# Instruction order and PSUM banks of a fused attention and gated-MLP kernel: a stored table in place of a list scheduler

## Chip, cores and metric

The kernel runs on one NeuronCore of one Trainium2 chip. The metric is the device time of one execution in microseconds. An execution is a little longer than the span of its profile, which runs from the first to the last recorded instruction.

## The reference

```python
# q, k, v: batch 4, heads 8, sequence 1152, head size 64 (fp32)
q_pool = q.reshape(B, H, S // 2, 2, D).mean(axis=3)          # 576 pooled queries
scores = (1 / sqrt(D)) * q_pool @ k^T
attn = softmax(scores)
x = (attn @ v), heads side by side                           # 2304 tokens x 512
gate = sigmoid(x @ w_gate); val = x @ w_val                  # 512 -> 1536
out = (gate * val) @ w_out                                   # 1536 -> 512
```

## The kernel before

**Tiling.** 32 heads are worked in 16 pairs, and four pairs make a batch. The 576 pooled queries of a head fall into two halves of 288, and its 1152 keys into nine chunks of 128. For fp32 accuracy, operands are split into a high and a low fp32r part. A chunk of scores is two matmuls (L610) into one PSUM bank; the first works on `QA`, `KA`, the second on `QB`, `KB`, whose rows also subtract the row maximum. Row maxima come from separate products of 384 columns (L504; L412 for the first head; L504 on `KP`, `QP` for the last 64 queries of a pair), each reduced by VectorE (L510, L417), and are put into `QB` as a diagonal (L335).

**Attention.** In the first batch (heads 0 to 7) ScalarE makes one exponential per chunk (L614, tile `e`), and three chunks at a time are multiplied with `ve` in plain fp32 (L628). In the later batches it makes two, a rounded one into `eh` (L614) and an exact one in place in the bank (L643); VectorE forms the difference `el` (L646). `eh` and `el` are multiplied with `vt` in products of their own (L653, L657), accumulating in two banks. The sums of the exponentials are added up on GpSimd (L675 to L685) and brought in by the two matmuls of L730 on `dh`.

**Gated MLP.** `gated` works on one batch at a time: products of twelve matmuls of 288 columns (L846, in four operations of three each) with the weights `wg`, then with `wo`. ScalarE (tanh, L889), VectorE (L895, L931) and GpSimd (L903) finish them. The MLP of one batch runs beside the attention of the next; behind the last batch only MLP is left. Weights are converted once (`convert`), stored to HBM and loaded again each time by SyncE. Eighteen filler operations (`busy`, L949; four matmuls of 192 columns each, L951) depend on nothing but one memset.

**What sets the order.** Every piece of work is handed to a planner, `pl.op(engine, duration, function, priority, after, uses, take)`, and every buffer is a `Hold` of a tag with so many slots. `Plan.run` (L92) is a list scheduler: it starts the ready operation of the lowest priority number on each engine that is free, by hand-written durations, and gives a buffer the slot that is free the longest. `Plan.search` (L66, called at L1000) repeats this 30 times with shifted priorities. An operation counts as ready when all of `after` and the first user of each of its buffers are done; a buffer counts as free when all its users are done. The operations are then issued in the order found (L1001), under `manual_schedule`. The waits between engines are put in afterwards, from what each instruction reads and writes. TensorE, ScalarE, VectorE, GpSimd and SyncE (which issues nearly all DMAs) each run their own instructions in that order. The eight PSUM banks are the tag `b`; every other tag takes its slots in turn.

Of the kernel before, what the change touches and what calls it, by code (L numbers as in the profile page):

```python
# [22 lines left out]

class Op:
    def __init__(self, eng, dur, fn, prio, after=(), take=None, late=0.0, keep=0.0, behind=None):
        self.eng, self.dur, self.fn, self.prio = eng, dur, fn, prio
        self.after = [a for a in after if a is not None]
        self.take, self.late, self.keep = take, late, keep
        self.users, self.start, self.end, self.behind, self.next = [], None, None, behind, []


class Hold:


    def __init__(self, tag, first=None):
        self.tag, self.slot, self.ops = tag, None, []


class Plan:


    WAIT = 0.4
    LAT = {"PE": 0.2, "ACT": 0.16, "DVE": 0.14, "POOL": 0.1, "SP": 0.0}

    def __init__(self, slots, free_order=()):
        self.free_order = free_order
        self.ops = []
        self.slots = slots
        self.holds = {t: [] for t in slots}
# [6 lines left out]
    def op(self, eng, dur, fn, prio, after=(), uses=(), take=(), late=0.0, keep=0.0, behind=None):  # L56
        o = Op(eng, dur, fn, prio, after, list(take), late, keep, behind)
        for h in uses:
            if behind is None:
                o.after.append(h.ops[0])  # L60
        for h in list(take) + list(uses):
            h.ops.append(o)
        self.ops.append(o)
        return o

    def search(self, rounds, width, shift):  # L66
        dice = random.Random(1)
        best = self.run()
        end = max(o.end for o in best)
        made = [(o, o.start, o.end) for o in best]  # L70
        slots = [(h, h.slot) for hs in self.holds.values() for h in hs]
        for _ in range(rounds):
            at = dice.uniform(-width, end)
            near = [(o, o.prio) for o, s, _ in made if at <= s <= at + width and o.eng != "SP"]
            for o, p in near:
                o.prio = p + dice.uniform(-shift, shift)
            order = self.run()
            new = max(o.end for o in order)
            if new <= end:
                best, end = order, new  # L80
                made = [(o, o.start, o.end) for o in best]
                slots = [(h, h.slot) for hs in self.holds.values() for h in hs]
            else:
                for o, p in near:
                    o.prio = p
        for o, a, b in made:
            o.start, o.end = a, b
        for h, s in slots:
            h.slot = s
        return best  # L90

    def run(self):  # L92
        n_dep = {}
        ready = {e: [] for e in self.LAT}
        for o in self.ops:
            o.users, o.next = [], []
        for k, o in enumerate(self.ops):
            o.key = (o.prio, k)
            o.at = 0.0
            n_dep[o] = len(o.after)  # L100
            for a in o.after:
                a.users.append(o)
            if o.behind:
                n_dep[o] += 1
                o.behind.next.append(o)
        free = {t: [(0.0, s) for s in range(n)] for t, n in self.slots.items()}
        nxt = {t: 0 for t in self.slots}
        left, of = {}, {}
        for t, hs in self.holds.items():
            for k, h in enumerate(hs):  # L110
                h.k, h.end = k, 0.0
                left[h] = len(h.ops)
                for o in h.ops:
                    of.setdefault(o, []).append(h)
        for o in self.ops:
            if n_dep[o] == 0:
                heapq.heappush(ready[o.eng], (o.key, o))
        busy = {e: 0.0 for e in self.LAT}
        done, order, t = 0, [], 0.0
        times = [0.0]  # L120
        heapq.heapify(times)
        seen = set()

        def can(o, t):
            for h in o.take:
                n = sum(g.tag == h.tag for g in o.take) if h.tag in self.free_order else 1
                if (h.tag not in self.free_order and nxt[h.tag] != h.k) or sum(f <= t + 1e-9 for f, _ in free[h.tag]) < n:
                    return False
            return True

        while done < len(self.ops):
            if not times:
                left = sorted((o.key[0], o.eng) for e in ready for _, o in ready[e])
                raise RuntimeError(f"planner stuck at {t}: {left[:10]} {nxt}")
            t = heapq.heappop(times)
            while times and times[0] <= t + 1e-9:
                heapq.heappop(times)
            again = True
            while again:
                again = False  # L140
                for e in self.LAT:
# [896 lines left out]
```

## Time and profile before

| | |
|---|---|
| median of 3 runs | 920.66 us (920.31 to 920.88) |
| span of the profiled execution | 919.1 us |
| TensorE matmuls | 910.0 us busy, 99% of the span, 6371 instructions |
| TensorE weight loads | 882.8 us, 96% |
| VectorE / ScalarE / GpSimd | 71% / 72% / 73% |

The page lists no other time for the profiled execution than its span, so the difference between the median and the span, 1.6 us, is taken as what lies around the span. A matmul's recorded duration (about 295 ns for 288 columns) is longer than the distance from one start to the next (about 133 ns), because matmuls are pipelined. So the cadence, instructions per time, says more than the busy share.

### The profile page before, as it was taken

How to read it: one execution, taken by the hardware profiler on the slowest of the kernel's cores; microseconds unless marked ns; L12 is line 12 of the kernel's file. 1: busy time of each engine (PE TensorE's matmuls, PEld its weight loads, DVE VectorE, ACT ScalarE, POOL GpSimd, SP SyncE). 2: the span in 40 equal slices, each digit the busy share in tenths (PEclk: the TensorE clock that was granted, in tenths of full speed). 3: DMA queues.
4: the chain of work that ended last, by engine and by line, in shares of the span. 5: the costliest groups of instructions: out<-in, count | busy, mean ns of one | idle time of the engine just before them, and what ended most of it. 6: DMA issues, size and time to landing. Idle time of an engine off the chain costs nothing.

```text
span 919.1 us, 18605 instructions
## 1 busy us (share of the span) xinstructions
PE 910.0 (99%) x6371; PEld 882.8 (96%) x6371; DVE 649.5 (71%) x1427; ACT 657.5 (72%) x1703; POOL 671.1 (73%) x669
## 2 busy tenths in 40 slices
PE   8999999999999999999999999999999999999998
PEld 8888888999999999999999999999999999999998
DVE  6677779888898987878787878877777874510112
ACT  4798899989998886777887677677877767422111
POOL 6765366889888989889899888888889877521211
PEclk9999999999999999999999999999999999999999
DMA  6899888788868666555644455554545423435432
GB/s 140 212 289 247 275 254 261 239 266 273 262 210 275 206 202 192 161 157 149 166 136 142 131 157 157 160 148 132 166 123 158 142 93 115 166 139 183 162 115 75
DMA packets 57616, 166.27 MB, mean 181 GB/s; under 512 B 17393, under 2 KB 21745, under 8 KB 51377
## 3 DMA queue, kind: packets, MB, share of 16 engines
q1 hardware_dynamic: 57360, 164.78, 59.3%
q8 instruction: 50, 0.82, 0.4%
q10 hardware_dynamic: 160, 0.30, 0.1%
q14 instruction: 46, 0.37, 0.1%
HBM read 132.12 MB, written 23.59 MB: 169 GB/s over the span
## 4 chain that ended last, share of the span: by engine, by line
PE 91%; ACT 4%; DVE 3%; POOL 1%; DMA 1%; issue 1%; POOLq 0%; ACTq 0%; DVEq 0%
PE bank L846 47%; PE bank L610 15%; PE bank L504 7%; PE bank L628 7%; PE bank L657 6%; PE bank L653 6%; PE bank L730 1%; DVE pm L417 1%; PE bank L951 1%; DMA wg<-wg_d 1%; ACT eh L614 1%; ACT bank L643 0%; ACT KA L475 0%; DMA wo<-wo_d 0%; DVE el L646 0%
## 5 line engine op out<-in xcount | busy, mean ns | idle before, releaser
L846 PE MATMUL bank<-x,wg 128*128 128x288 f32 x2304 | 353.8, 295 | 0.0
L846 PEld LDWEIGHTS bank<-x,wg 128*128 128x128 f32 x2304 | 325.6, 188 | 1.1 <-ACT sg L889 0.4
L646 DVE TENSOR_TENSOR el<-bank,eh 128x288 fp32r<-128x288 f32 x432 | 192.9, 452 | 70.7 <-ACT bank L643 65.9
L510 DVE TENSOR_REDUCE pm<-bank 128x1 f32<-128x384 f32 (+1 forms) x375 | 199.7, 550 | 49.6 <-PE bank L504 45.0
L614 ACT ACTIVATE eh<-bank 128x288 fp32r<-128x288 f32 x432 | 176.4, 409 | 73.1 <-PE bank L610 65.9
L643 ACT ACTIVATE bank<-bank 128x288 f32<-128x288 f32 x432 | 176.9, 410 | 0.2
L610 PE MATMUL bank<-QA,KA 128*128 128x288 f32 x576 | 175.1, 308 | 1.5 <-DVE pm L510 0.9
L610 PE MATMUL bank<-QB,KB 128*128 128x288 f32 x576 | 167.4, 295 | 0.0
L903 POOL TENSOR_TENSOR g<-sg,g 128x288 fp32r<-128x288 f32 x96 | 79.9, 833 | 105.2 <-ACT g L899 102.7
L675 POOL TENSOR_TENSOR acc<-acc,eh 128x576 f32<-128x576 f32 x92 | 132.5, 1440 | 16.7 <-ACT eh L614 14.6
L846 PE MATMUL bank<-g,wo 128*128 128x288 f32 x864 | 139.2, 295 | 0.2
L657 PE MATMUL bank<-el,vt 128*128 128x288 f32 x432 | 127.2, 296 | 0.5 <-DVE el L646 0.5
L653 PE MATMUL bank<-eh,vt 128*128 128x288 f32 x432 | 127.3, 296 | 0.0
L846 PEld LDWEIGHTS bank<-g,wo 128*128 128x128 f32 x864 | 125.0, 188 | 1.2 <-DMA wo<-wo_d 0.3
L504 PE MATMUL bank<-KA,QA 128*128 128x384 f32 (+1 forms) x375 | 125.7, 350 | 0.2
L610 PEld LDWEIGHTS bank<-QA,KA 128*128 128x128 f32 x576 | 108.2, 188 | 5.9 <-DVE pm L510 1.3
L610 PEld LDWEIGHTS bank<-QB,KB 128*128 128x128 f32 x576 | 108.3, 188 | 1.3
L895 DVE SCALAR_TENSOR_TENSOR sg<-sg,bank 128x288 f32<-128x288 f32 x96 | 43.3, 451 | 81.2 <-PE bank L846 79.2
L657 PEld LDWEIGHTS bank<-el,vt 128*128 128x128 f32 x432 | 81.1, 188 | 1.5 <-DVE el L646 1.2
L653 PEld LDWEIGHTS bank<-eh,vt 128*128 128x128 f32 x432 | 81.1, 188 | 0.7 <-ACT eh L614 0.3
L675 POOL TENSOR_TENSOR acc<-eh,eh 128x576 f32<-128x576 f32 x48 | 68.7, 1431 | 15.6 <-ACT eh L614 10.9
L628 PE MATMUL bank<-e,ve 128*128 128x288 f32 x288 | 76.6, 407 | 0.0
(86 smaller groups left out, 1359.6 us busy)
## 6 DMA issues: line engine op xcount, KB each, us to landing
wg<-wg_d SPq DMA_DIRECT2D x48, 1024.0 KB, 5.2
wo<-wo_d SPq DMA_DIRECT2D x36, 512.0 KB, 3.9
kr<-in_kT_dram SPq DMA_DIRECT2D x62, 288.0 KB, 5.0
wg_d<-cs SPq DMA_DIRECT2D x24, 512.0 KB, 5.0
qr<-in_qT_dram SPq DMA_DIRECT2D x31, 288.0 KB, 4.1
KP<-KA SPq DMA_DIRECT2D x30, 288.0 KB, 4.4
vr<-in_v_dram SPq DMA_DIRECT2D x24, 288.0 KB, 3.1
cr<-in_wg_dram SPq DMA_DIRECT2D x12, 512.0 KB, 5.3
```

The lines of the kernel that those rows point to most:

```text
L504: nc.tensor.matmul(out=tl(m)[LO if t == 4 else ALL, 0:384], lhsT=lhs(t), rhs=rhs()[:, j * 384:(j + 1) * 384], start=True, stop=True)
L510: nc.vector.tensor_reduce(out=o, in_=tl(m)[p, 0:384], axis=AXX, op=ALU.max)
L610: nc.tensor.matmul(out=tl(m)[:, 0:GN], lhsT=tl(hd["k"])[k][:, ks], rhs=tl(hd["q"])[k][:, a:b], start=(k == 0), stop=(k == 1))
L614: nc.scalar.activation(out=ev(), in_=tl(m)[:, 0:GN], func=ACTF.Exp, scale=1.0 / 16.0)
L628: nc.tensor.matmul(out=tl(av[0])[:, 0:GN], lhsT=pair(c, 0), rhs=tl(h), start=(c == 0), stop=(c == NC - 1))
L643: nc.scalar.activation(out=p, in_=p, func=ACTF.Exp, scale=1.0 / 16.0)
L646: nc.vector.tensor_tensor(out=tl(el), in0=tl(m)[:, 0:GN], in1=ev().bitcast(F32), op=ALU.subtract)
L653: nc.tensor.matmul(out=tl(av[0])[:, 0:GN], lhsT=pair(c, w), rhs=ev(), start=(c == 0), stop=(c == NC - 1))
L657: nc.tensor.matmul(out=tl(av[1])[:, 0:GN], lhsT=pair(c, 1 - w), rhs=tl(el), start=(c == 0), stop=(c == NC - 1 and not mine_c))
L675: nc.gpsimd.tensor_tensor(out=tl(acc), in0=tl(old).bitcast(F32), in1=tl(eh).bitcast(F32), op=ALU.add)
L846: nc.tensor.matmul(out=ps[:, 0:GN], lhsT=l, rhs=r, start=(n == 0 and j == 0), stop=(n == 3 and j == 2))
L903: nc.gpsimd.tensor_tensor(out=g[:, 1, a:b], in0=tl(sg), in1=g[:, 0, a:b].bitcast(F32), op=ALU.subtract)
```

## The change

The scheduler is removed, and two constants take its place. Unpacked, `ORDER` holds 7153 numbers, a permutation of all operations as the code creates them; `PLACES` holds 3069 slots, one for each buffer hold. Operations, their instructions and their operands stay as they are, and so does the issue under `manual_schedule`, with waits derived from reads and writes.

Set against the order before, engine by engine: of TensorE's 3141 operations 3015 stand at another place, by 9 places on average and at most 62. Of ScalarE's 1703, 1486 are moved (4 places on average), of VectorE's 1348, 1185 (3), of GpSimd's 624, 544 (4), of SyncE's 337, 265 (2, at most 13). 1266 of 1448 PSUM holds sit in another bank; no slot of another tag differs. The order keeps to the true reads and writes and no longer to every `after` and buffer rule of the code. For instance, an `el` product may stand before the `eh` product of the same chunk, and a bank is taken by its first real writer.

```diff
-import heapq
-import random
+import base64
+import zlib
...
+ORDER = (
...
+)
+PLACES = (
...
+)
 class Op:
-    def __init__(self, eng, dur, fn, prio, after=(), take=None, late=0.0, keep=0.0, behind=None):
...
+    def __init__(self, eng, fn, after=()):
+        self.eng, self.fn, self.after = eng, fn, [a for a in after if a is not None]
...
     def op(self, eng, dur, fn, prio, after=(), uses=(), take=(), late=0.0, keep=0.0, behind=None):
-        o = Op(eng, dur, fn, prio, after, list(take), late, keep, behind)
-        for h in uses:
-            if behind is None:
-                o.after.append(h.ops[0])
+        o = Op(eng, fn, list(after) + [behind])
...
-    def search(self, rounds, width, shift):
...
-    def run(self):
...
+    def placed(self):
+
+        order = [self.ops[k] for k in unpack(ORDER, "H")]
+        holds = [h for t in self.slots for h in self.holds[t]]
+        for h, s in zip(holds, unpack(PLACES, "B"), strict=True):
             h.slot = s
+        assert len(set(order)) == len(self.ops) == len(order)
+        assert all(h.slot < self.slots[h.tag] for h in holds)
         return order
+
+
+def unpack(text, kind):
+    return list(memoryview(zlib.decompress(base64.b85decode(text))).cast(kind))
...
-    order = pl.search(30, 30.0, 1.0)
+    order = pl.placed()
     with tc.manual_schedule():
```

What the unpacked table says at the places of which the prediction speaks:

| | before | table |
|---|---|---|
| filler operations on TensorE ahead of the first maximum product (L412) | 8 | 15 |
| filler operations between the last L412 and the first score product | 4 | 0 |
| first-head reductions (L417) ahead of the first diagonal | 9 | 10 |
| `el` products with under 2.5 us of TensorE work between them and their scores, of 432 | 34 | 2 |
| the same distance for `el` / `eh` products, median | 3.0 / 2.7 us | 6.4 / 8.7 us |
| the same for L730 behind what its sums were made from, median | 6.2 us | 8.5 us |
| banks of a maximum product taken again within 1.25 us of TensorE work, of some 400 | 23 | 71 |
| smallest TensorE work between the last use of a `wg` buffer and its next use | 12.1 us | 6.8 us |
| the same for the last batch's `wo` tiles, which lie in `KA` | 5.2 us | 4.4 us |

"TensorE work" is counted along TensorE's order with the cadences of the trace (133 ns for 288 columns, 175 ns for 384, 242 ns for a plain fp32 matmul).

## Rows read from the trace of the kernel before

**Rows 1.** Page, its head and part 1: busy time, share of the span, instructions.
```profile
span 919.1 us, 18605 instructions
PE 910.0 (99%) x6371; PEld 882.8 (96%) x6371; DVE 649.5 (71%) x1427; ACT 657.5 (72%) x1703; POOL 671.1 (73%) x669
```
**Rows 2.** Page, part 4: the chain that ended last, by engine.
```profile
PE 91%; ACT 4%; DVE 3%; POOL 1%; DMA 1%; issue 1%; POOLq 0%; ACTq 0%; DVEq 0%
```
**Rows 3.** The same chain in order of time: start, length, what, count.
```profile
23.68 1.21 PE bank L504 x7
28.65 2.91 PE bank L628 x12
798.75 117.15 PE bank L846 x882
```
**Rows 4.** Groups by line: busy us, mean ns, idle before; for the counts.
```profile
L628 PE MATMUL bank<-e,ve 128*128 128x288 f32 x288 | 76.6, 407 | 0.0
L504 PE MATMUL bank<-KA,QA 128*128 128x384 f32 (+1 forms) x375 | 125.7, 350 | 0.2
L504 PE MATMUL bank<-KP,QP 128*128 128x384 f32 x45 | 15.6, 356 | 0.0
L412 PE MATMUL bank<-KA,QA 128*128 128x384 f32 (+1 forms) x15 | 3.9, 346 | 0.0
L951 PE MATMUL bank<-sel 128*128 128x192 f32 x72 | 12.5, 334 | 2.7 <-DVE sel L991 2.7
```
**Rows 5.** Busy time of each engine by stage, all instructions, counts in brackets.
```profile
200.00:400.00 200.00, 198.75 (x1438) 195.24 (x1437) 174.04 (x380) 169.39 (x441) 179.56 (x174) 1.00 0.73 222
400.00:800.00 400.00, 399.61 (x2932) 396.46 (x2931) 302.05 (x673) 297.22 (x801) 340.90 (x335) 1.00 0.47 143
800.00:916.00 116.00, 115.89 (x875) 115.66 (x873) 18.75 (x42) 24.15 (x57) 20.18 (x25) 1.00 0.39 136
```
**Rows 6.** The same stages, L504 alone: matmuls, then weight loads.
```profile
200.00:400.00 200.00, 32.40 (x100) 18.26 (x100) 1.00 0.73 222
400.00:800.00 400.00, 57.45 (x180) 32.79 (x180) 1.00 0.47 143
```
**Rows 7.** TensorE's own waits: us in total, times, longest.
```profile
PE bank L951 <- DVE sel L991: 2.7, 1, 2.7
PE bank L610 <- DVE pm L510: 0.9, 1, 0.9
PE bank L730 <- POOL dh L726: 0.7, 2, 0.5
PE bank L657 <- DVE el L646: 0.5, 2, 0.3
PE bank L610 <- ACT e L614: 0.5, 1, 0.5
```
**Rows 8.** Timeline of the first 17 us: start, length, engine, line, count.
```profile
2.73 7.01 PE L951 MATMUL bank<-sel 128*128 128x192 f32 x32 [2.73 <-DVE sel L991]
9.58 0.72 PE L412 MATMUL bank<-KA,QA 128*128 128x384 f32 x3
9.98 4.32 DVE L417 TENSOR_REDUCE pm<-bank 128x1 f32<-128x384 f32 x9 [3.37 <-PE bank L412]
14.61 0.72 DVE L335 TENSOR_TENSOR QB<-ident,pm 64x192 fp32r<-64x192 f32 x2
14.88 1.93 PE L951 MATMUL bank<-sel 128*128 128x192 f32 x16
16.65 0.31 PE L610 MATMUL bank<-QA,KA 128*128 128x288 f32 x1
```
**Rows 9.** DMA issues: count, KB each, median us from issue to landing.
```profile
wg<-wg_d SPq DMA_DIRECT2D x48, 1024.0 KB, 5.2
KA<-wo_d SPq DMA_DIRECT2D x12, 512.0 KB, 3.3
```
**Rows 10.** Line L481, the low half of K: durations, min/median/max in ns.
```profile
L481 DVE TENSOR_TENSOR KB<-kr,KA x16: 755/963/1925, 323.5 to 727.3; 64x576 fp32r<-64x576 f32 x16
```

More of the change, by code (lines that the diff above doesn't have):

```diff
@@ L32, with __init__ @@
+class Op:
+    def __init__(self, eng, fn, after=()):
+        self.eng, self.fn, self.after = eng, fn, [a for a in after if a is not None]
 class Hold:
-    def __init__(self, tag, first=None):
+    def __init__(self, tag):
         self.tag, self.slot, self.ops = tag, None, []
 class Plan:
-    WAIT = 0.4
-    LAT = {"PE": 0.2, "ACT": 0.16, "DVE": 0.14, "POOL": 0.1, "SP": 0.0}
     def __init__(self, slots, free_order=()):
-        self.free_order = free_order
         self.ops = []
@@ L64, in op @@
         return o
-    def search(self, rounds, width, shift):
[L67 to L88, printed above, removed]
-            h.slot = s
-        return best
@@ L92, in run @@
-    def run(self):
[L93 to L141, printed above, removed]
-                    if busy[e] > t + 1e-9:
-                        continue
-                    put, pick, soon = [], None, []
-                    while ready[e]:
-                        it = heapq.heappop(ready[e])
-                        o = it[1]
-                        if o.at <= t + 1e-9 and can(o, t):
-                            pick = o
-                            break
-                        if t < o.at <= t + self.WAIT and can(o, o.at):
-                            soon.append(o)
-                        put.append(it)
-                    if pick and e != "PE" and any(
-                        t + pick.dur > u.at + self.WAIT and u.prio < pick.prio - 0.3 for u in soon
-                    ):
-                        heapq.heappush(ready[e], it)
-                        pick = None
-                    for it in put:
-                        heapq.heappush(ready[e], it)
-                    if pick is None:
-                        continue
-                    o = pick
-                    for h in o.take:
-                        h.slot = min((s for s in free[h.tag] if s[0] <= t + 1e-9), key=lambda s: s[0])[1]
-                        free[h.tag] = [s for s in free[h.tag] if s[1] != h.slot]
-                        nxt[h.tag] += 1
-                    o.start, o.end = t, t + o.dur
-                    busy[e] = o.end
-                    order.append(o)
-                    done += 1
-                    again = True
-                    heapq.heappush(times, o.end)
-                    av = o.end + self.LAT[e] + o.late
-                    for h in of.get(o, ()):
-                        left[h] -= 1
-                        h.end = max(h.end, av + o.keep)
-                        if left[h] == 0:
-                            free[h.tag].append((h.end, h.slot))
-                            heapq.heappush(times, h.end)
-                    for u in o.users + o.next:
-                        n_dep[u] -= 1
-                        u.at = max(u.at, o.end if u.behind is o or u.eng == e and not o.late and e != "SP" else av)
-                        if n_dep[u] == 0:
-                            heapq.heappush(ready[u.eng], (u.key, u))
-                            heapq.heappush(times, u.at)
-        return order
```

160 lines of the change are left out of this document (156 added, 4 removed).

## The prediction

> **What bounds the kernel now.** I read the busy shares first: TensorE's matmuls fill 99% of the span, the other three compute engines 71 to 73% [rows 1]. The chain that ended last says the same from the other side: 91% of it is TensorE's own work [rows 2]. So only two things can move the end: work that TensorE is given, and time in which it runs slower than its cadence. The change gives it the same 6371 matmuls, so all turns on the second. The busy share hides that time: a matmul is recorded as 0.29 us long while the next starts 0.13 us later, so a delay of up to 0.16 us leaves no idle gap. I therefore count cadences.
>
> In the last stretch TensorE works alone: 882 matmuls of 288 columns in 117.15 us, 132.8 ns each; a plain fp32 one (L628) takes 2.91 / 12 = 242 ns, one of 384 columns 1.21 / 7 = 173 ns [rows 3]. The counts: 288 of L628, 375 + 45 + 15 of 384 columns, 72 fillers [rows 4]; the rest of 6371, 5576, have 288 columns. Undisturbed, the work without fillers takes 5576 x 0.1328 + 435 x 0.173 + 288 x 0.2425 = 740.5 + 75.3 + 69.8 = 885.6 us. The 15 maximum products of the first head (2.6 us) come ahead of the first score product at 16.65 us [rows 8], so 883.0 us stand behind it. There it has until 798.75 + 117.15 = 915.90 us [rows 3], which is 899.2 us. **TensorE loses 16.2 us behind 16.65.** The stages show where: from 200 to 400 us, 1338 matmuls of 288 columns and 100 of L504 need 177.7 + 17.3 = 195.0 of 200 us, 5.0 lost; from 400 to 800, 365.5 + 31.1 = 396.6, 3.4 lost; behind 800 nothing [rows 5, 6]. The remaining 8 us lie before 200.
>
> By the busy share there would be only 919.1 - 910.0 = 9.1 us to gain, of which 2.7 are the first wait and about 3.2 the last store [rows 1, 7]. The Trainium skill (Perfetto Trace Analysis, Identifying the Most-Contended Engine) says that matmul busy time is a poor measure and that weight-load busy time should be taken. That would leave 919.1 - 882.8 = 36 us here, which is too much, since the fp32 products have fewer weight loads per time. My sum uses neither.
>
> **What the change removes, and its price.** The planner ran on the host; taking it out costs or saves nothing on the chip. Instructions, operands and DMA sizes are the same, so the price of every operation is taken as it was. Left are the places.
>
> *First stretch.* The first 32 filler matmuls start at 2.73 us and L412 follows at 9.58: 214 ns each. Later 16 of them take from 14.88 to 16.65, 111 ns each [rows 8]: TensorE runs at half its later rate until about 9.5 us, although it is fed without a pause. The table puts 15 filler operations, 60 matmuls, ahead of the first L412. The first 32 are the same instructions at the same time, so I let them take the same 6.85 us; 28 more at 111 ns are 3.1 us. L412 then starts at 12.7 instead of 9.58. VectorE's reductions hang on it: nine took 4.32 us, 0.48 each [rows 8]; the table puts ten ahead of the diagonal, 4.8. With 0.4 us to the first reduction and the 1.0 us of the two small steps (14.30 to 15.33), the diagonal is done at 12.7 + 0.4 + 4.8 + 1.0 = 18.9. Before, it was done at 15.33, but 16 fillers stood in the way until 16.65; the table has none there. So the score products start near 19.0, **2.4 us later**. Nothing hides this, since TensorE is the bound behind it. Bounds: if all 60 fillers ran at 111 ns, L412 would start at 9.4 and the scores 0.8 us earlier than now; with an extra wait in the refilled pipeline it is 3.1. I take +2.4, by the nearest row.
>
> *Score products to their consumers.* The waits of TensorE that show as idle are 2.6 us without the first: 1.2 for `dh` and `el`, which are results made from scores, 1.4 for a maximum and an exponential on which a score product waits [rows 7]. I divide the 16.2 us in this ratio, 7.5 and 8.7, since the short waits have no row of their own. The table pulls the first kind apart: the products on `el` stand 6.4 us of TensorE work behind their scores instead of 3.0 (median), 2 instead of 34 within 2.5 us; L730 stands 8.5 instead of 6.2 behind. ScalarE, VectorE and GpSimd have idle time in every stage (from 200 to 400 us VectorE is busy 174 of 200 [rows 5]), so twice the distance covers a late difference. I let this kind go, -7.5; bounds 0 and -7.5.
>
> *Banks.* Wider distances hold `eh`, `el` longer, and banks are retaken sooner: 71 instead of 23 retakings of a maximum's bank within 1.25 us. A matmul (0.35 us), a reduction (0.48 us) [rows 4, 8] and two hand-overs fit into 1.25 us only if VectorE turns to it at once. On the other side first-head and second-head operands come earlier on ScalarE, and a bank is free from its last real reader on. I take -0.5 for the 8.7 us of this kind; bounds -7 (nearly all gone) and +11 (the slower rival).
>
> *Queues.* SyncE's loads move by 2 places on average. The `wg` buffers' smallest reload distance falls from 12.1 to 6.8 us of TensorE work, against 5.2 us to landing; the `KA` tiles of the last batch have 4.4 against 3.3 [rows 9]. Their cover is these 1.6 and 1.1 us; a load queued behind another's wait by more than that costs TensorE the excess, some 2 us each. I price it at nothing. At the end the last product, VectorE's step and the store keep their order: nothing.
>
> **Sum.** 919.1 + 2.4 - 7.5 - 0.5 = 913.5 us of span; with the 1.6 us between the span and the median of the runs, **915.1 us**: 8 of the 16.2 us saved, 2.4 given back.
>
> **Rivals.**
> *More of it goes (chance 0.2).* If the bank kind falls by 5 to 7 us as well, the span is 919.1 + 2.4 - 7.5 - 6 = 908, the time 909.6. For it: behind 400 us the old order already loses only 3.4 in 400 us [rows 5, 6], so a nearly tight order exists on this chip. Against it: that was the stretch with the least conversion work, and part of the loss is unevenness of the cadence, which no order removes.
> *No change (0.19).* The late start eats the gain: if only 1 to 4 us of the loss go, +2.4 leaves 919 to 922, about 920.5. For it: an order tuned to durations as recorded once does not carry them along. VectorE's low half of K took between 755 and 1925 ns [rows 10]. The Trainium skill (SBUF — State Buffer, Who interferes with whom) has a rule that speaks against fixed durations: a VectorE instruction with two SBUF inputs contends with a GpSimd instruction that reads SBUF, and the earlier one decides who waits. By that rule a new order makes new pairs, and the 1925 ns would turn up at other places. By the row, 16 instructions times at most 1 us are at stake on an engine with 26 us idle in 200, so alone it gives this rival, not the next.
> *Slower (0.16).* The place is the maximum's bank. Of the 2.6 us of visible waits 0.9, 35%, is a score product behind a maximum; 35% of 16.2 is 5.6 us. If that grows as the close retakings do, 71 / 23, it becomes 17, +11.6. Then 919.1 + 2.4 - 7.5 + 11.6 = 925.6, the time 927. It decides from +5.1 us on, where it uses up the gain. Against it: at 1.25 us a free VectorE still arrives in time.
> That the table does not act as written (waits put in by slot rather than by reads and writes, which would set the earlier `el` products behind the old holds) I give 0.03 and count under slower. A score product that starts while another bank is read shows that banks are kept apart.
>
> **How the numbers follow.** The forecast has 0.42, the bigger gain 0.2, no change 0.19, slower 0.19. What a measurement can tell here is about 0.2%, 1.8 us. Faster by more than that (under 918.8) are the first two, 0.62; within it 0.19; slower 0.19. The forecast's own range is 912 to 918.5. Eight in ten reach from the middle of the bigger gain, 909.5, past no change to the foot of the slower case, 923.5.
>
> **What would show it.** Right: the first L412 starts near 12.7 us and the first L610 near 19; TensorE's loss behind that, by the same count, is about 8 us; its waits for `el` and `dh` are gone from its list; more matmuls fit between 200 and 400 us than 1438. Wrong: L610 still near 16.6, so the fillers cost nothing; or TensorE's waits name maxima (L510) or weights in place of `el`; or the loss is still 16 us. The prediction falls with the step on the first stretch if the fillers reach their fast cadence at another time, and with the step on banks if the waits named are mostly banks.

## The result: slower, and the profile after

The table takes 932.77 us (median of four runs, 930.85 to 936.89); the kernel before, run beside it, took 920.48. The ratio is 1.0137, 95% interval 1.011 to 1.0163: 1.4% slower, where 915.1 was forecast. The profiled execution took 931.0 us with a span of 929.2, 10.1 more than before. In the changed kernel's line numbers, and so in its profile, everything from L300 on stands 40 lines lower: L610 is L650, L646 `el` is L686, L504 is L544, L846 is L886, L481 is L521, L465 is L505, L335 is L375.

The page's head and part 1 (busy time, share, instructions), to be held against [rows 1]:

```profile
span 929.2 us, 18567 instructions
PE 908.1 (98%) x6371; PEld 883.0 (95%) x6371; DVE 654.1 (70%) x1427; ACT 654.8 (70%) x1703; POOL 668.9 (72%) x669
```

The same 6371 matmuls, two microseconds less of busy time, ten more of span. The stages tell where (columns as in [rows 5]: window, its length, then busy us and count of PE, PEld, DVE, ACT, POOL, then TensorE's granted clock, DMA share, GB/s):

```profile
16.60:50.00 33.40, 30.92 (x160) 27.24 (x159) 24.91 (x54) 24.30 (x57) 21.39 (x19) 0.95 0.67 161
200.00:400.00 200.00, 197.75 (x1440) 195.22 (x1439) 171.48 (x378) 169.52 (x442) 178.31 (x174) 1.00 0.70 217
400.00:800.00 400.00, 392.68 (x2876) 388.94 (x2875) 304.02 (x663) 293.85 (x800) 334.83 (x330) 1.00 0.46 140
```

By the prediction's own count, 200 to 400 us holds 1340 x 0.1328 + 100 x 0.173 = 195.2 us of work: 4.8 lost, before 5.0. From 400 to 800 it holds 2696 x 0.1328 + 180 x 0.173 = 389.2: **10.8 us lost, before 3.4**. Behind 800 us nothing is lost, as before. The last long piece of the chain (start, length, what, count) ends at 926.04:

```profile
813.27 112.77 PE bank L886 x849
```

That is 907.3 us behind the first complete score (18.72, below) for 883.0 us of work: 24.3 lost instead of 16.2. With 4.8 and 10.8 taken out, 8.7 lie ahead of 200 us, where the old order had 7.8. So the 10.1 us are 2.1 of later start, 0.9 ahead of 200 us and 7.4 between 400 and 800, less 0.2 between 200 and 400 (10.2 with rounding).

TensorE's own waits behind the first one (us in total, times, longest), against [rows 7]:

```profile
PE bank L650 <- DVE el L686: 3.8, 2, 2.7
PE bank L650 <- DVE QB L375: 2.0, 1, 2.0
PE bank L650 <- ACT sg L929: 1.7, 1, 1.7
PE bank L544 <- DVE pm L550: 1.7, 2, 1.0
PE bank L544 <- DMA KP<-KA: 1.3, 1, 1.3
PE bank L544 <- DVE el L686: 1.2, 2, 0.8
PE bank L886 <- DVE el L686: 1.0, 2, 0.8
```

The `el` and `dh` products (L657, L730 before) no longer wait for their operands. In their place score, maximum and MLP products wait for `el`, 6.0 us together. None of them reads `el`: they want the **bank** that the subtraction `el` still reads. And these are few and long, where the old order's list has 2.6 us of waits behind the first one and its other losses show in the cadence alone. They are no accident of one execution: in the profiles of e6 and e10 (below) the longest stands at the same place, 2.7 us both times.

The longest, in the timeline (start, length, engine, line; what the engine waited for stands in brackets):

```profile
592.71 3.79 DVE L505 TENSOR_TENSOR QA<-qr,QA 64x576 fp32r<-64x576 f32 x1
593.09 1.43 POOL L612 TENSOR_TENSOR vt<-vr,vt 128x576 fp32r<-128x576 f32 x1
594.49 1.39 POOL L715 TENSOR_TENSOR acc<-acc,eh 128x576 f32<-128x576 f32 x1
595.96 1.19 POOL L722 TENSOR_TENSOR acc<-acc 128x288 f32<-128x288 f32 x1
596.53 0.56 DVE L550 TENSOR_REDUCE pm<-bank 128x1 f32<-128x384 f32 x1
597.00 0.45 DVE L686 TENSOR_TENSOR el<-bank,eh 128x288 fp32r<-128x288 f32 x1
597.51 0.40 PE L650 MATMUL bank<-QA,KA 128*128 128x288 f32 x1 [2.74 <-DVE el L686]
```

VectorE's low half of Q takes 3.79 us. It ends only when two GpSimd operations of 1.4 us, with two inputs each, have passed beside it and a third has begun. Behind it on VectorE wait a maximum, then `el`, and behind `el` a bank for TensorE. All durations of this operation and its twin for K (min/median/max in ns):

```profile
L521 DVE TENSOR_TENSOR KB<-kr,KA x16: 755/1196/2039, 322.6 to 757.0; 64x576 fp32r<-64x576 f32 x16
L505 DVE TENSOR_TENSOR QA<-qr,QA x16: 751/1186/3789, 317.5 to 734.9; 64x576 fp32r<-64x576 f32 x16
```

For K the median was 963 before [rows 10], for Q 770:

```profile
L465 DVE TENSOR_TENSOR QA<-qr,QA x16: 751/770/1736, 319.3 to 718.8; 64x576 fp32r<-64x576 f32 x16
```

Summed over the 32, they took 31.6 us before and 42.9 after; all 32 at their shortest would be 24.1. `el` itself, with one input in PSUM, has no such spread: its median is 449 ns, its longest 460.

The first stretch, against [rows 8]:

```profile
2.73 9.81 PE L991 MATMUL bank<-sel 128*128 128x192 f32 x60 [2.73 <-DVE sel L1031]
12.38 0.54 PE L452 MATMUL bank<-KA,QA 128*128 128x384 f32 x2
12.96 4.72 DVE L457 TENSOR_REDUCE pm<-bank 128x1 f32<-128x384 f32 x10 [5.92 <-PE bank L452]
16.36 0.40 PE L650 MATMUL bank<-QA,KA 128*128 128x288 f32 x1
17.86 0.71 DVE L375 TENSOR_TENSOR QB<-ident,pm 64x192 fp32r<-64x192 f32 x2
18.72 0.37 PE L650 MATMUL bank<-QB,KB 128*128 128x288 f32 x1 [1.97 <-DVE QB L375]
```

The first half of the first score, on `QA` and `KA`, already runs at 16.36; its second half, on `QB`, waits for the diagonal. Behind that 2 us wait the clock is down. In this row of the stages (PE, PEld, DVE, ACT, POOL, clock as above) the granted clock is 0.54 of 2.4 GHz, so nearly all of the stretch ran at the lower level, 1.2 GHz, and the score products start every 240 ns instead of every 133:

```profile
18.70:22.30 3.60, 3.58 (x16) 3.60 (x17) 3.52 (x10) 1.90 (x5) 0.88 (x1) 0.54 0.04 8
```

### The profile page after: what moved, and what is told of

The parts are those of the page before. It is cut to its first block, busy times and chain, and to the rows that moved or that the text cites. A ratio compares the mean times of both kernels' runs of the same rounds, so it can differ in the third digit from the quotient of the medians.

```text
span 929.2 us, 18567 instructions
## 1 busy us (share of the span) xinstructions
PE 908.1 (98%) x6371; PEld 883.0 (95%) x6371; DVE 654.1 (70%) x1427; ACT 654.8 (70%) x1703; POOL 668.9 (72%) x669
## 4 chain that ended last, share of the span: by engine, by line
PE 86%; DVE 5%; ACT 3%; DMA 2%; issue 2%; POOL 1%; SPq 0%; DVEq 0%; ACTq 0%; POOLq 0%
PE bank L886 44%; PE bank L650 15%; PE bank L544 7%; PE bank L668 7%; PE bank L697 5%; PE bank L693 5%; PE bank L770 1%; PE bank L991 1%; DMA wg_d<-cs 1%; DVE KB L521 1%; ACT eh L654 1%; DMA KP<-KA 1%; DVE el L686 1%; ACT bank L683 1%; DMA wo_d<-cs 1%
## 5 line engine op out<-in xcount | busy, mean ns | idle before, releaser
L886 PE MATMUL bank<-x,wg 128*128 128x288 f32 x2304 | 373.8, 295 | 0.8 <-DVE el L686 0.8
L886 PEld LDWEIGHTS bank<-x,wg 128*128 128x128 f32 x2304 | 331.5, 188 | 1.6 <-DVE y L752 1.2
L550 DVE TENSOR_REDUCE pm<-bank 128x1 f32<-128x384 f32 x375 | 199.3, 551 | 52.8 <-PE bank L544 47.6
L686 DVE TENSOR_TENSOR el<-bank,eh 128x288 fp32r<-128x288 f32 x432 | 186.4, 451 | 55.6 <-ACT bank L683 42.7
L650 PE MATMUL bank<-QA,KA 128*128 128x288 f32 x576 | 175.1, 310 | 6.2 <-DVE el L686 3.8
L683 ACT ACTIVATE bank<-bank 128x288 f32<-128x288 f32 x432 | 169.9, 407 | 0.2
L650 PE MATMUL bank<-QB,KB 128*128 128x288 f32 x576 | 167.3, 296 | 2.0 <-DVE QB L375 2.0
L886 PE MATMUL bank<-g,wo 128*128 128x288 f32 x864 | 147.5, 295 | 0.3 <-DVE el L686 0.2
L886 PEld LDWEIGHTS bank<-g,wo 128*128 128x128 f32 x864 | 127.5, 188 | 1.3 <-DVE y L752 0.6
L544 PE MATMUL bank<-KA,QA 128*128 128x384 f32 x375 | 122.1, 350 | 3.0 <-DVE pm L550 1.7
L650 PEld LDWEIGHTS bank<-QA,KA 128*128 128x128 f32 x576 | 109.2, 190 | 11.2 <-DVE el L686 4.5
L697 PE MATMUL bank<-el,vt 128*128 128x288 f32 x432 | 117.5, 296 | 1.2 <-DVE cs L847 0.5
L650 PEld LDWEIGHTS bank<-QB,KB 128*128 128x128 f32 x576 | 109.3, 190 | 3.5 <-issue 2.2
L693 PE MATMUL bank<-eh,vt 128*128 128x288 f32 x432 | 110.6, 295 | 0.0
L935 DVE SCALAR_TENSOR_TENSOR sg<-sg,bank 128x288 f32<-128x288 f32 x96 | 43.1, 450 | 93.5 <-PE bank L886 58.9
L929 ACT ACTIVATE sg<-bank 128x288 f32<-128x288 f32 x96 | 39.2, 411 | 54.8 <-PE bank L886 49.7
```

The costliest lines, as they stand in the source:

```text
L544: nc.tensor.matmul(out=tl(m)[LO if t == 4 else ALL, 0:384], lhsT=lhs(t), rhs=rhs()[:, j * 384:(j + 1) * 384], start=True, stop=True)
L550: nc.vector.tensor_reduce(out=o, in_=tl(m)[p, 0:384], axis=AXX, op=ALU.max)
L650: nc.tensor.matmul(out=tl(m)[:, 0:GN], lhsT=tl(hd["k"])[k][:, ks], rhs=tl(hd["q"])[k][:, a:b], start=(k == 0), stop=(k == 1))
L683: nc.scalar.activation(out=p, in_=p, func=ACTF.Exp, scale=1.0 / 16.0)
L686: nc.vector.tensor_tensor(out=tl(el), in0=tl(m)[:, 0:GN], in1=ev().bitcast(F32), op=ALU.subtract)
L693: nc.tensor.matmul(out=tl(av[0])[:, 0:GN], lhsT=pair(c, w), rhs=ev(), start=(c == 0), stop=(c == NC - 1))
```

## The experiments

The kernel before took 920.3 to 920.9 us (medians) beside every experiment. Where two kernels other than before are compared, it is by their medians; the table's own four runs lie 6 us apart, so such a difference is good to some 2 or 3 us only.

**What the order loses on VectorE: one input in place of two.** In the table (e2) and in the old order (e3) the 32 low halves are reductions of one element each, the same size with one SBUF input. Both leave out the low halves of these operands.

```diff
-            e = nc.gpsimd if on == "POOL" else nc.vector
+            if on != "POOL":
+                nc.vector.tensor_reduce(out=qa[HI, 0:SQ], in_=tl(qr)[:, 0].unsqueeze(2), axis=AXX, op=ALU.max)
+                return
+            e = nc.gpsimd
```

(and the same for K)

> The table, with the 32 low-half subtractions on VectorE (QA, KB of the later heads) replaced by an operation of the same size that reads one SBUF tensor instead of two (a maximum over one element); the low halves of those operands are left out by it. Theory of contention: these 32 operations, 0.75 us when undisturbed and up to 3.8 us in the table's run, wait for GpSimd's reads; what follows them in VectorE's queue comes late, and the table has no slack there. Then they take 0.6 to 0.8 us each without exception, TensorE's loss from 400 to 800 us falls from some 10 us to under 4, and the time falls by 6 to 8 us to about 925. Rival, that the sooner retaken banks alone make the loss: the durations become short but at least 7 of the 10 us stay and the time is within 2 us of the table's.

> The kernel before with the same replacement of the 32 subtractions on VectorE (their low halves left out). Control: under the theory of contention the old order has slack around them, so it gains little, 0 to 2 us, 918.5 to 920.5. If it gains 6 us as well, the order has nothing to do with it.

e2 took 923.66 us (ratio to before 1.003, 1.0009 to 1.0052), 9.1 less than the table; e3 took 916.73 (0.9954, 0.9938 to 0.9971), 3.9 less than before. The spread of the operation is gone in e2:

```profile
L524 DVE TENSOR_REDUCE KB<-kr x16: 743/750/753, 326.2 to 750.8; 64x576 fp32r<-64x576 f32 x16
L505 DVE TENSOR_REDUCE QA<-qr x16: 745/746/747, 321.6 to 728.7; 64x576 fp32r<-64x576 f32 x16
400.00:800.00 400.00, 399.59 (x2943) 397.61 (x2943) 294.10 (x674) 297.43 (x807) 332.54 (x337) 1.00 0.48 145
```

From 400 to 800 it fits 2943 matmuls in place of 2876, and TensorE's waits for `el` fall from 6.0 to 0.6 us in all. So the two inputs cost the table 9.1 us and the old order 3.9; what the new order adds by them is the difference, 5.2. Without them the table is still 6.9 us slower than the old order (923.7 against 916.7), so there are other causes as well.

One thing more goes with this edit. The reduction doesn't read the high half, so VectorE no longer waits for ScalarE to make it. In the table it did so ahead of five of the 32, 4.6 us in all; in the old order ahead of none. The table's own trace tells the two apart. From 400 to 800 us TensorE has six waits of over 0.4 us, and ahead of each VectorE works with no gap over 0.1 us from one or two of these subtractions to the operation that releases TensorE (us; the excess is counted over 0.755 for each subtraction):

| TensorE's wait ends at | its length | subtractions just ahead | their excess | VectorE's wait for a high half ahead of them |
|---|---|---|---|---|
| 448.16 | 1.04 | 1.91, 1.25 | 1.65 | 0.33 |
| 502.43 | 1.06 | 1.47, 1.87 | 1.83 | 1.43 |
| 597.51 | 2.74 | 3.79 | 3.03 | none |
| 640.42 | 0.45 | 2.01 | 1.25 | none |
| 668.81 | 0.82 | 1.66, 1.88 | 2.03 | 0.75 |
| 708.78 | 0.65 | 2.04 | 1.28 | none |

In all six the excess alone is longer than TensorE's wait; the wait for the high half is so in one. How the losses too short to show as waits divide between the two isn't told by this.

**Is it length, or unevenness?** The same reductions with every element read twice, 1.35 us each, 43.1 us together: as much as the uneven 42.9 of the table. Again without the low halves. The edit is that of e2 and e3, with this line in it (and the same for K):

```diff
+                nc.vector.tensor_reduce(out=qa[HI, 0:SQ], in_=tl(qr)[:, 0].unsqueeze(2).to_broadcast([64, SQ, 2]), axis=AXX, op=ALU.max)
```

> The kernel before with the 32 VectorE operations replaced by undisturbed ones of twice the elements (one SBUF tensor read, low halves left out): every one takes the same 1.3 to 1.4 us instead of 0.75 in e3, 19 us more on VectorE in all. Theory of slack: the old order has room around them, and loses 1 to 3 us against e3's 916.7, to 918 to 920. Rival, that both orders are equally tender and the table's operations were only stretched more: it loses as much as the table does in e8.

> The same operations of twice the elements in the table's order. Theory of slack: the table places VectorE's next results so closely behind them that it loses more than the old order does, 5 to 9 us against e2's 923.7, to 929 to 933. Rival: the same 1 to 3 us as e7 against e3, 925 to 927.

The old order took 922.05 (+5.3 against e3), the table 927.93 (+4.3 against e2). The operation in e8:

```profile
L524 DVE TENSOR_REDUCE KB<-kr x16: 1343/1350/1352, 321.7 to 752.4; 64x576 fp32r<-64x1152 f32 x16
```

That the table has less slack on VectorE and so suffers more from any lengthening isn't borne out: both suffer alike, within the noise. But the same sum unevenly spread costs the table 932.8, 4.8 us more than evenly spread. The old order says the same: 7.5 us of uneven lengthening (31.6 less 24.1) cost it 3.9, 19.2 us of even lengthening 5.3. In both orders a microsecond of lengthening costs about twice as much where it comes uneven. That the unevenness alone does this isn't shown: e7 and e8 have none of GpSimd's additions lengthened (next experiment), and e8 lacks the waits for the high half as well.

**What lengthens them.** The two engines alone, the whole computation left out. Its calls, with two sizes added:

```diff
+nc.vector.tensor_tensor(out=c[HI], in0=a[HI], in1=b[HI], op=ALU.subtract)      # 64x576
+nc.vector.tensor_reduce(out=m[HI], in_=a[HI].unsqueeze(2), axis=AXX, op=ALU.max)
+nc.vector.tensor_tensor(out=n[HI], in0=a[HI, 0:64], in1=b[HI, 0:64], op=ALU.mult)
+nc.gpsimd.tensor_tensor(out=z, in0=x, in1=y, op=ALU.add)                       # 128x576
+nc.gpsimd.memset(w, 0.0)
```

> A kernel of its own, of the two engines alone: it leaves out the whole computation, so its time says nothing; only the durations of its parts are read. On VectorE stand a subtraction with two SBUF inputs (64x576), a reduction of the same size with one, and a small product with two (64x64); on GpSimd an addition with two SBUF inputs (128x576) and a memset of the same size. Seven parts, set apart by waits between the two engines: the subtraction alone; the addition alone; subtraction beside addition; subtraction beside memset; reduction beside addition; small product alone; small product beside addition. Theory (a VectorE instruction with two SBUF inputs is held up by GpSimd reading SBUF): subtraction 0.75 us alone and beside the memset, above 1.0 us on average and uneven beside the addition; reduction 0.75 beside the addition; small product about 0.22 us alone and for some up to 1.4 us, the length of one addition, beside it. Rival (any work of GpSimd, or the load on SBUF as a whole, stretches it): the memset stretches the subtraction too, or the reduction beside the addition is longer than 0.75 us. If the subtraction is never stretched here, the cause in the kernel is not GpSimd.

The answers by line for the parts in turn (min/median/max in ns): the subtraction alone, beside additions, beside memsets; the addition alone, beside subtractions, beside reductions; the small product alone, beside additions.

```profile
L29 DVE TENSOR_TENSOR c<-a,b x12: 755/755/756, 4.8 to 13.5; 64x576 fp32r<-64x576 f32 x12
L29 DVE TENSOR_TENSOR c<-a,b x14: 755/1839/1839, 35.6 to 58.9; 64x576 fp32r<-64x576 f32 x14
L29 DVE TENSOR_TENSOR c<-a,b x14: 755/755/756, 62.2 to 72.4; 64x576 fp32r<-64x576 f32 x14
L38 POOL TENSOR_TENSOR z<-x,y x14: 1396/1397/1397, 14.9 to 34.0; 128x576 f32<-128x576 f32 x14
L38 POOL TENSOR_TENSOR z<-x,y x14: 1793/1794/1928, 35.7 to 60.2; 128x576 f32<-128x576 f32 x14
L38 POOL TENSOR_TENSOR z<-x,y x14: 1396/1400/1410, 80.3 to 99.5; 128x576 f32<-128x576 f32 x14
L35 DVE TENSOR_TENSOR n<-a,b x20: 222/222/223, 101.1 to 105.9; 64x64 fp32r<-64x64 f32 x20
L35 DVE TENSOR_TENSOR n<-a,b x13: 222/1441/1442, 106.6 to 123.0; 64x64 fp32r<-64x64 f32 x13
```

The subtraction is lengthened by GpSimd's additions alone, from 755 to 1839 ns; memsets leave it at 755. A reduction and an addition leave each other as they are. The reductions beside additions, in the page's row (busy us, mean ns, idle before):

```profile
L32 DVE TENSOR_REDUCE m<-a 64x576 fp32r<-64x576 f32 x14 | 10.5, 749 | 0.5
```

The small product takes 1441 in place of 222 ns, about the length of an addition. The Trainium skill (SBUF — State Buffer, Who interferes with whom) says just this: two SBUF inputs on VectorE contend with GpSimd's reads, and neither GpSimd's writes nor a VectorE instruction with one input does. This run agrees on these three points.

**Queues.** The put of `KP` stands on SyncE ahead of the K load that it had been queued behind, and every third weight conversion has a third `cs` buffer (a free part of an `x` tile); e9 adds the one-input reductions, without the low halves.

```diff
+put, load = self.ops[295], self.ops[406]
+order.remove(put)
+order.insert(order.index(load), put)
...
+    h.third = k < 28 and k % 3 == 2
```

> The table, with two waits taken away by what makes them wait: a third buffer for the converted weights (a tile of x that is free till then) for every third conversion, so that ScalarE no longer waits behind a store of 5 to 9.5 us to land, and the second copy into KP issued ahead of the K load of a later head instead of behind it. Theory of the queues: the stalls of TensorE at 50.8 us (1.3 us), 190.8 (1.9) and 222.7 (0.6) come from DMAs on which an engine's queue waits, and go: 3 to 4 us off the table's 932.8, more where the stall at 190 had let the clock fall. Rival, that these stalls come from the banks: they stay within 20%, and the time within 1 us.

> The table with the one-input operations of e2 (low halves left out) and the two queue edits of e6. If contention and queues are separate causes, their gains add: e2's 923.7 less the 2.7 us that e6 gained, about 921, and TensorE's stalls at 50.8 and 190 us are gone from e2's list. If the queue stalls were only a consequence of contention, it stays at e2's 923.7.

e6 took 930.08 (1.01, 1.0083 to 1.0117), 2.7 less than the table, where the two intervals just touch; e9 took 919.63 (0.999, 0.9976 to 1.0004), 4.1 less than e2. The stalls at 50.8 us (1.3) and 190.8 us (1.7) are gone from both; the one at 222.7 us gave way to others of 0.9 us (e6, for a `wo` load) and 1.0 us (e9). In the table's chain, in order of time, they are these landings:

```profile
42.88 7.51 DMA KP<-KA
179.07 9.46 DMA wg_d<-cs
```

The usual time to landing is 5.2 us for the put and 5.4 for the store.

**The start.** e1 leaves eight of the eighteen filler operations ahead of the first maximum product and puts ten behind maximum products; e5 puts five in between and five behind the last maximum ahead of the scores; e4 is e1 with one-input reductions, without the low halves. The banks of four products are exchanged to keep the order of their users.

The lines of e5:

```diff
+        busy, ahead = order_busy(order), 8
+        rest = busy[ahead:]
+        order = [o for o in order if o not in set(rest)]
...
+        for m, o in zip([maxima[k] for k in (1, 4, 5, 9, 11, 13, 13, 13, 13, 13)], rest):
+            order.insert(order.index(m) + 1, o)
```

> The table, with its filler operations put back as they stood before: eight ahead of the first maximum product, ten between the later ones; everything else in the table's order (four banks of the first head are exchanged so that the fillers keep theirs). Theory of the start: seven filler operations too many delay the first maximum by 2.8 us, and the 2.2 us wait that follows lets the clock fall. Then L412 starts near 9.6 us, the first score products run at the full cadence of 133 ns, TensorE's granted clock stays 1.00, the runs scatter by under 1 us instead of 6, and the time falls by 3 to 5 us against the table, to 928 to 930. Rival, that the start is absorbed by later waits: the scores come earlier, the time stays within 1 us of the table's.

> The table with both edits, the fillers as before and the one-input operations (low halves left out). If the two theories are right and add up, 10 to 11 us go: about 921, TensorE's loss behind the first score product 10 to 13 us. If the order is at fault in some other way, 924 or more stays.

> The table with another place for the fillers. In e1 a filler operation behind each maximum product held the maxima back, so the diagonal was still late (first QB product at 18.22 us) and the clock fell again; e1 did not test the start. Here eight filler operations stand ahead of the first maximum, five between the maxima and five behind the last one that precedes the scores. Theory of the start: VectorE's reductions then run without a gap from 9.6 us, the QB product starts at 15.5 to 16.5, the score products run at 133 ns, the granted clock stays 1.00 from there to 50 us, and TensorE's loss up to 50 us is 6 to 7 us instead of 9.9: 3 to 4 us off the table's 932.8. Rival: it is absorbed later, under 1 us.

Neither e1 nor e5 helped. e1 took 934.14 (1.0142, 1.0117 to 1.0168): the first maximum product came at 9.16 us, but the fillers between held back the later ones, and the first `QB` product came at 18.22. e4 took 920.67 (1.0011, 0.999 to 1.0031), 3.0 less than e2, but the intervals of the two overlap (e2 from 1.0009 on), so that the fillers count where the contention is gone isn't shown by it. e5 took 934.18 (1.0137, 1.0107 to 1.0166): there the diagonals were late (line L387, min/median/max in ns).

```profile
L387 DVE TENSOR_TENSOR QB<-ident,pm x4: 540/1368/1520, 15.6 to 21.4; 64x192 fp32r<-64x192 f32 x2, 64x64 fp32r<-64x64 f32 x2
L390 DVE TENSOR_TENSOR QB<-ident,pm x1: 1305/1305/1305, 23.0 to 23.0; 64x64 fp32r<-64x64 f32 x1
```

They too have two SBUF inputs; the 64x64 product takes 222 ns alone, as above. Moved earlier, they fall beside GpSimd's conversions of the second head. So e10 takes e6, the fillers of e5 and the first head's diagonals on ScalarE; e11 adds the one-input reductions, without the low halves.

```diff
+nc.scalar.activation(out=q[1][LO, 128 * t + 64 * par:128 * t + 64 * par + 64], in_=ident[p, p],
+                     func=ACTF.Copy, scale=o[p, t, 3:4])
```

> The table with e6's queue edits, e5's fillers, and the diagonals of the first head made by ScalarE (a copy with a factor per partition) instead of VectorE; everything is computed. In e5 the fillers were right, but VectorE's diagonals, which read two SBUF tiles, took 2.03 and 2.79 us instead of 0.72 and 0.45, beside GpSimd's work for the next heads, which the table has put there. Theory: with ScalarE, which reads through a port of its own, they take what they take alone, 1.3 us at most for the first six, the QB product starts before 16.8 us, TensorE's loss up to 50 us is 4.5 to 6.5 us (8.0 in e6), and the time is 926 to 928. Rival, that the start of the table is late for another reason: the loss stays at 8 or more.

> All edits: e10 with the one-input operations (low halves left out). If the three causes, start, queues and contention, are all that makes the table slower, it comes to e3's level, the old order with the same one-input operations, 916 to 918. What is left above 918 is a cause not found yet; under 916 the table's order is better than the old one once its durations hold.

In e10 the first `QB` product starts at 16.7, as early as before (16.8), yet the time is 929.45 (1.0093, 1.008 to 1.0107), hardly less than e6. **e11 took 914.09 (0.9931, 0.9917 to 0.9945)**: 5.5 less than e9, and 2.6 less than the old order with the same reductions (e3), though that lacks the other edits of e11 and the two intervals overlap. So the start is worth 5.5 us once these contended operations are gone, and 0.6 while they are there. What e11 mends in e9 is two waits in the first 25 us, the second for a 64x64 diagonal that took 1.31 us:

```profile
PE bank L666 <- DVE QB L385: 2.2, 1, 2.2
PE bank L666 <- DVE QB L388: 2.1, 1, 2.1
```

The late diagonals are two-input operations as well, so part of what is booked here as start is contention again. e10's rows of the stages show where the gain went; columns as above, the clock third from the end:

```profile
325.90:329.00 3.10, 3.10 (x15) 3.10 (x14) 0.52 (x2) 0.84 (x3) 0.29 (x1) 0.50 0.14 51
594.00:599.00 5.00, 4.38 (x20) 4.38 (x21) 4.29 (x10) 1.78 (x5) 2.47 (x4) 0.66 0.61 132
```

Both follow on a wait of TensorE, 2.0 us for a `wg` load and 2.7 us for `el`. In the first the granted clock is 0.50: all of it at the lower level, 15 matmuls in 3.1 us.

**What fewer fillers do to the old order.** The old kernel without its last three filler operations.

```diff
-            pl.op("PE", 0.7 if k < 6 else 0.36, busy, -5 + 0.01 * k, uses=[bz] if k else [], take=[] if k else [bz])
+            pl.op("PE", 0.7 if k < 6 else 0.36, busy if k < 15 else lambda: None, -5 + 0.01 * k, uses=[bz] if k else [], take=[] if k else [bz])
```

> The kernel before without the last three of its eighteen filler operations (12 matmuls), everything computed. The diagonal of the first head is done at 15.33 us, and the first score product waits for fillers until 16.65. Theory: it starts 1.0 to 1.3 us sooner and all behind it too, 919.0 to 919.6. Rival, that TensorE finds no work so early and waits later, or the clock falls in the short gap: 920.4 or more.

920.18 us (0.9996, 0.9987 to 1.0005): no change. The first diagonals came 1.3 us earlier, and the first complete score 2.15; before and then e12:

```profile
16.80 0.30 PE L610 MATMUL bank<-QB,KB 128*128 128x288 f32 x1
```

```profile
14.65 0.37 PE L610 MATMUL bank<-QB,KB 128*128 128x288 f32 x1 [0.34 <-DVE QB L335]
```

But then the diagonals, like e5's, took up to 1474 ns where before none took over 355. TensorE's order is the same in both kernels but for the fillers, so the same matmul can be compared: the 61st, fillers not counted, starts at 24.73 us instead of 25.49, so by then 0.8 of the 2.15 us are left.

**Can the contention be had out with everything computed?** One way is that VectorE doesn't do the subtraction. In the old kernel all 32 go to GpSimd (e14), or the 16 of K alone (e16); the planner makes a new order.

```diff
-        on = "POOL" if QLP(u) else "DVE"
+        on = "POOL"
...
-            by = "DVE" if k and KLD(u) else "POOL"
+            by = "POOL"
```

> The kernel before with all 32 VectorE subtractions of two SBUF inputs (low halves of Q and K) given to GpSimd, everything computed; the planner makes a new order for it. If the 3.9 us that the old order gained with one-input instructions came from VectorE being held up by GpSimd, and GpSimd has room (it is 85% busy from 400 to 800 us), the time falls to about 917. If GpSimd, which takes 1.43 us for each, 46 us more, becomes the engine that TensorE waits for, the time is above 922 and TensorE's waits name KA or KB, dh or QB.

> The same with the 16 subtractions of K alone on GpSimd, 23 us more for it. Contention halved and room kept: about 918.5. If new orders of the planner scatter by more than that gain, the time is anywhere from 917 to 923 and says nothing on contention.

e14 took 937.05 (1.0172, 1.0157 to 1.0187); **e16 took 918.52 (0.9976, 0.9967 to 0.9986), faster than both kernels** by a quarter of a per cent. The stage from 400 to 800 us, e14 and then e16:

```profile
400.00:800.00 400.00, 397.36 (x2856) 387.33 (x2855) 274.64 (x637) 292.05 (x794) 361.88 (x355) 1.00 0.46 138
```

```profile
400.00:800.00 400.00, 399.53 (x2948) 398.28 (x2947) 293.36 (x665) 298.71 (x801) 356.29 (x350) 1.00 0.48 145
```

GpSimd is busy 362 of 400 us in e14, 356 in e16, 341 before. e16 fits 16 matmuls more than before, e14 76 fewer. TensorE's waits in e14 don't name GpSimd's tiles in the lead (the largest behind the start is 1.7 us for `eh`), so that GpSimd has become what sets its pace is likely from its load, not shown. e16's gain came with a new order, and another order of the planner's may scatter by as much. Nor did it do away with much contention. The 16 subtractions of Q that VectorE kept:

```profile
L465 DVE TENSOR_TENSOR QA<-qr,QA x16: 752/1092/1710, 322.5 to 725.7; 64x576 fp32r<-64x576 f32 x16
```

They took 18.0 us, 6.0 over their shortest, where all 32 had 7.5 over it before. The 2 us may as well come from the 16 us of work that VectorE no longer does. What made e16 faster is open.

## Why the prediction was wrong, step by step

**What bounds the kernel** held. TensorE is the bound, the loss is read by cadence, and the 2.1 + 8.1 us found that way add up to the 10.1 of the span, within rounding.

**First stretch (+2.4): right in place and size, incomplete.** The first L452 was put at 12.7 and came at 12.38, the reductions at 4.8 and took 4.72, the score at 19.0 and came complete at 18.72: +2.1. (By the letter the first L650 came at 16.36, near the sign of being wrong; it is the half that doesn't need the diagonal. The lower bound, 0.8 us earlier, is 0.9 by its own terms.) It left out the clock: the sum took the products behind the wait at their full rate; 16 of them ran at 240 ns instead of 133, 1.7 us more. And "Nothing hides this" isn't borne out. In e12 the old order's scores began 2.15 us sooner, and the time stayed; in e10 they began 1.7 us sooner than in e6 (16.68 against 18.34), for 0.6 us. Between e9 and e11 the start as a whole measured 5.5 us.

**Scores to consumers (-7.5): right about the waits named, wrong about the sum.** These waits are gone, but the loss from 200 to 400 fell by only 0.2 us, from 5.0 to 4.8. Dividing the 16.2 us in the ratio of the visible waits was the weak step: the waits for `el` went from TensorE's operands to its banks. In e11, whose queues and start are mended, the table's order beats the old one with the same reductions (e3) by 2.6 us, a third of what was put down, and even that isn't clear of the noise.

**Banks (-0.5, bounds -7 and +11): sign wrong, and the wrong bank.** The slower rival put its price on the banks of maxima. Products waiting for a maximum's reduction make up 2.3 us of the waits after; those for banks held by `el` make up 6.0. The rival was right that there would be loss by banks retaken too soon, wrong in whose, and in why: with VectorE in time (e2) the waits for `el` are 0.6 us.

**The step that failed** is, before the others, the premise that "the price of every operation is taken as it was", with the sentence that let contention go: "16 instructions times at most 1 us are at stake on an engine with 26 us idle in 200, so alone it gives this rival, not the next". It is 32 instructions, since Q's low halves have the same form (L465); the largest was 3.0 us over, not 1; and where the sum has no term, e2 prices the two inputs at 9.1 us in the table, against 3.9 in the old order (e3). Idle time over 200 us is no cover for a bank that is wanted at once. The Trainium skill's rule that the prediction named there was the right one, and it was weighed by a sum where the place of each instance counts.

**Queues (priced at nothing): mis-sized.** The covers of 1.6 and 1.1 us for `wg` and `KA` held in the table's own profile, where neither is among the waits; elsewhere they didn't always, as in e10, where a `wg` load cost 2.0 us once, the "some 2 us each" of the forecast. The put of `KP` and the stores of converted weights had not been looked at, and they cost 2.7 us (e6), 4.1 without the contention.

**How the miss divides.** From the table downwards the runs give 932.8 as it is, 923.7 without the lengthened subtractions, 919.6 with the queues mended as well, 914.1 with the start mended too; the old order gives 920.5, and 916.7 with the same one-input operations. So the 12.3 us by which the table is slower are contention 9.1 - 3.9 = 5.2, queues 4.1, start 5.5 and the rest of the order -2.6. The sum had 0, 0, +2.4 and -8.0 in these places. The shares depend on the sequence, since the causes overlap: with queues (2.7) and start (0.6) mended first, e10 to e11 leaves 15.4 for the two inputs, 11.5 more than in the old order. Each number is good to some 2 or 3 us.

That e11's 914.1 lies near the forecast's 915.1 is luck, not a late confirmation: e11 leaves out the low halves, begins its scores 0.5 us late and not 2.4 (its first `QB` product starts at 17.29 us), has a third buffer and ScalarE for the diagonals, and the old order's 916.7 in e3 is what it is to be held against.

## What to carry to other kernels

An order tuned on recorded durations is only as good as their constancy: ahead of freezing it, list the operations whose max is far from their min, and find out what they share with the engine beside them. A bank or buffer waits for the single latest release, so look at such an operation's longest instance and at what is queued behind it, not only at its mean and the engine's idle share. Where instructions of two engines lengthen each other, give one of them a form with one input, or let one engine do both pieces of work, as far as it has room (with all 32 on GpSimd, e14 got slower). And an earlier start is worth only what the next operations leave of it.

## What the runs showed of the hardware

A VectorE subtraction of 64x576 with two SBUF inputs takes 0.755 us alone and beside GpSimd memsets, 1.839 beside back-to-back GpSimd additions, and once 3.79 in the kernel. The addition is lengthened too, from 1.397 to 1.794. A 64x64 product goes from 0.222 to 1.441, so here the price is the length of GpSimd's instruction. Beside each other the subtraction and the addition take 1.79 us a pair (25.1 us for 14), less than the 2.15 of one behind the other, so there they still overlap in part.

A single wait of TensorE can cost more than its length: the clock may be lower behind it, in a kernel whose TensorE is 98% busy. It needn't be. The 2.7 us wait for `el` stands at the same place in the profiles of the table, e6 and e10. Behind it e6 is granted 0.50 over 5.2 us and e10 0.66 over 5 us, as shown; the table has its full clock:

```profile
597.50:601.00 3.50, 3.49 (x25) 3.50 (x26) 3.44 (x7) 1.78 (x5) 2.11 (x3) 1.00 0.75 169
```

That it differs so between executions may be why the table's times lie 6 us apart and e11's 1.7. That was not tested.
